# Rows out of a spectral filter, scattered to experts one tile at a time instead of chunk by chunk

## The chip, the cores and the metric

The kernel runs on one core of a Trainium2 chip. Its engines are PE (matrix products), DVE and ACT (vector and scalar work), POOL (here mostly scatters) and SP (which issues transfers). The metric is the device time of one execution in microseconds (us); lower is better. The time before is 1450.88 us, the median of three runs (1448.48 to 1457.94).

## The reference, cut to what matters

Eight batches of 2496 tokens with 256 channels go through a filter in frequency space, and every row of the result then goes through one of eight experts, the one whose normalised embedding is nearest:

```python
def _attn_ref(x, filt_r, filt_i):                 # x: 8 x 2496 x 256
    X = np.fft.rfft(x, axis=1)
    F = (filt_r + 1j * filt_i)[None, :, :]
    return np.fft.irfft(X * F, n=x.shape[1], axis=1).astype(np.float32)

def _moe_ref(x, expert_emb, tau, w1, w2):         # x: 19968 x 256, 8 experts, 1024 hidden
    xn = x / (np.linalg.norm(x, axis=-1, keepdims=True) + 1e-06)
    en = expert_emb / (np.linalg.norm(expert_emb, axis=-1, keepdims=True) + 1e-06)
    logits = xn @ en.T / tau
    expert_idx = np.argmax(logits, axis=1)
    ...
    gate_w = probs[np.arange(N), expert_idx]      # softmax of the logits, at the largest
    for e in range(E):
        mask = expert_idx == e
        h = np.maximum(x[mask] @ w1[e], 0.0)
        out[mask] = gate_w[mask, None] * (h @ w2[e])
```

## The kernel before, in words

**Groups and stages.** Each batch is a group of its own; there are eight groups, 0 to 7. The filter of a group takes three steps: `conv_s1` (39-point transform along b), `conv_s2` (64-point transform along a, product with the filter, and back) and `conv_sb` (back along b). `conv_sb` works in 11 tiles of two halves of 117 rows each; a half is what the text calls a row tile of the scatter, and 22 of them make a group. For each tile it writes the rows as two 16-bit halves of a number into a `rows` tile, with the token's number from a POOL `iota` (L571), has them transposed by a transfer (`yT`, L537), and computes logits (L595).

**Routing.** After four tiles (a *chunk*; eight row tiles, in the last chunk of a group six) `route` does the rest for all of them at once on DVE: softmax, first largest expert, and the place of each row within its expert's region of the buffer `XS` in memory (`ix`, L664). The places are cast to integers `ixi` (L666), the output scales go into the rows (L678), and POOL scatters each row tile to `XS` with an indirect transfer (L687, `scatter_rows`). `route` is a generator, and `part()` in `conv_sb` advances it by one `yield`; `part()` is called twice for each tile, once per *half step*, and then until nothing is left. Between two `yield`s of `route` stand two scatters. There are 22 scatters per group in chunks of 8, 8 and 6, 176 in all, and eight more of empty rows at the end of group 7 (`zero_rows`).

**Slots.** When a group's filter ends, its rows are cut into *slots*, blocks of 256 rows of one expert (128 for the first group and for the last blocks). A slot loads its rows transposed (`xT`, by SP, from `XS`) and goes through its expert in four units (quarter slots). A unit has a copy of a quarter of the first weights on DVE (`wp`, L808, `prep`), the first product on PE (`ph`, L820), its positive part and remainder `h` on ACT (L826) and DVE (L827), and the second product on PE (`po`, L840). After the fourth unit ACT scales each 128 rows into a result tile `o` (L847), and POOL scatters it to the output (L848).

**What sets the order.** `run_slots` runs through the slots of all groups so far, and `spread`, called twice per unit, lays steps of the next group's filter between them: each step has a weight, and `pace` divides the steps' weight by the units that are left in the queue, so that the next group's filter ends just before the slots run out. PE's and ACT's instructions stay in the order of the program; DVE's, POOL's and SP's are ordered by a scheduler, which takes an instruction when its inputs are ready by its own reckoning. `behind("dve")` binds an instruction to a place behind the last weight copy issued so far (`last["dve"]`, set in `prep`). Pools hold the tiles: `rowp` 9 row tiles (a pool that the filter's parts `ap`, `yp` also use), `mp2` two of each of its tags, among them `o`.

Of the kernel before, what the change touches and what calls it, by code (L numbers as in the profile page):

```python
# [15 lines left out]
I32 = mybir.dt.int32  # L16
# [8 lines left out]
NA, NB39 = 64, 39          # sequence length 2496 = 64 * 39  # L25
S = NA * NB39
NK2 = 20                   # frequencies 0..19 of the 39-point transform
A3 = 3                     # a's in one token tile
TOK = A3 * NB39            # 117 tokens in a tile
NAG = (NA + A3 - 1) // A3  # 22 tiles in a batch, the last with one a  # L30
# [3 lines left out]
ROW = 516                  # hi 256, lo 256, token id, output scale  # L34
# groups of batches whose filter is done together; the rows of the slots that come after each
GROUPS = ((1, 128),) + ((1, 256),) * 7
CW = 2 * D                 # columns in a tile: two batches, or two places of one batch
CHUNK = 4                  # tiles of columns in a routing chunk
NTC = 2 * CHUNK
XYB, INB, CYB = 6, 4, 3    # buffers of the filter's products, of its inputs, of transposed rows  # L40
W_S1, W_S2, W_SB, W_GAP = 0.8, 1.0, 1.3, 2.5  # weights of the filter's steps between slots
MARGIN = 3                 # quarter slots that the filter of a group ends early
SAL, LPL = 2, 3            # tiles that lie between a step of the filter and the products that use it
# groups from which a transform takes its products by parts: there, back along b, a, and back along a
G_S1, G_SB, G_S2, G_SA = 2, 3, 4, 3
DLAG = 2                   # units between the two products of a unit
MID = 8                    # matrix products of a unit before the next slot's registers are loaded
WLOADS = {3: 1, 6: 1, 10: 2, 32: 2} | {n: 1 for n in range(12, 32, 2)}  # loads of weights at the first group's steps
WLATE = 6                  # experts whose halves follow their scales at once
PT = 1                     # half of a tile of the first group that the tensor engine transposes  # L50


def full_blocks(tokens, size):
    """Blocks of `size` rows that are full in E regions with `tokens` rows in all, at the least."""
    return max(0, -((E * (size - 1) - tokens) // size))
# [3 lines left out]
def moe_spectral_kernel(  # L59
# [25 lines left out]
    # phases: after which group, rows in a slot, slots  # L85
# [17 lines left out]
    rowp = ctx.enter_context(tc.tile_pool(name="rowp", bufs=9))  # L103
# [33 lines left out]
    # 8 - e, e * CAP, token ids, slot numbers  # L137
# [10 lines left out]
    # 1 where the partition holds a token, in a full tile and in the last one of a batch  # L148
# [9 lines left out]
    def norm_eps(out_, ssq, tmp):  # L158
        """sqrt(max(ssq, 1e-30)) + 1e-6 by Newton steps for the inverse root; ssq is clamped in place."""
# [25 lines left out]
    ent = const.tile([P, 2, 2 * E], F16, tag="ent", name="ent")   # per half of the channels: hi, lo  # L185
    enz = const.tile([P, 2, 2 * E], F16, tag="enz", name="enz")   # hi, 0
# [23 lines left out]
    def weight_loads():  # L210
        """The raw weights of an expert lie a place ahead of their halves, the last ones aside."""
# [16 lines left out]
    def weight_halves():  # L228
        """Powers of two that take the largest terms to [64, 128) and [2**14, 2**15); then the halves."""
# [57 lines left out]
    def tiles(g, t):  # L287
        """(batch, a-group) of the two halves of the t-th tile of columns."""
        n, _ = GROUPS[g]
        return [(first[g] + j, t) if n == 2 else (first[g], 2 * t + j) for j in range(2)]  # L290
# [4 lines left out]
    # e * CAP + rows so far  # L295
    state = {"base": ecap}

    def widths(g):
        """Tiles of columns in the transforms along b, and along a."""
        return NAG * GROUPS[g][0] // 2, NK2 * GROUPS[g][0] // 2  # L300


    def whole(g, ap, t, rows, full):
        """The parts of tile t of a tensor in memory: (half or both, partitions, memory)."""
# [38 lines left out]
    def split(hi, lo, pieces):  # L343
        """High and low parts of the pieces of a tile."""
# [13 lines left out]
    def asides(nm):  # L358
        """Room for parts in two tiles for rows."""
# [3 lines left out]
    def parts_of(c, tag):  # L363
        """A constant's high part in its place, and its low part."""
# [9 lines left out]
    def product(out_, c, a):  # L374
        """c times a tile's piece, in float32 or by parts."""
# [8 lines left out]
    def conv_s1(g):  # L384
        """39-point transform along b."""
# [19 lines left out]
    def conv_s2(g):  # L405
        """64-point transform along a, filter, and back."""
# [18 lines left out]
        def filtered(out_, in_, fts, ri):  # L425
            """in_ times the filter's real part, or times the sign and its imaginary part."""
# [21 lines left out]
        for k in range(NK + lag):  # L448
            if k + INB - 1 < NK:
                ain[k + INB - 1] = load_a(k + INB - 1)  # L450
            if k < NK:
# [6 lines left out]
                # real and imaginary halves change places  # L458
# [10 lines left out]
                else:  # L469
                    # while the first group is alone, the tensor engine has the time for the sum  # L470
# [22 lines left out]
    def conv_sb(g):  # L493
# [15 lines left out]
        def part():  # L509
            if parts and next(parts[0], None) is None:  # L510
                parts.pop(0)
# [530 lines left out]
```

## Time and profile before

| | |
|---|---|
| median of three runs | 1450.88 us (1448.48 to 1457.94) |
| profiled execution: span from first to last instruction | 1551.4 us |
| the profiled execution's own time | only its span is recorded, 100.5 us above the median |
| mean granted clock of PE | 0.901 |
| busy: PE, DVE, ACT, POOL | 83%, 64%, 48%, 36% |
| row scatters (L687) | 176, 179.2 us, 1018 ns each on average |
| result scatters (L848) | 161, 170.6 us, 1060 ns each |
| weight copies (L808) | 384, 190.8 us, 497 ns each |
| casts of places (L666) | 24, 0.166 us each (median) |

The profile is of one execution on the chip. Busy times are those of an engine's instructions; waits are idle times before an instruction with what ended them, its releaser. "issue" as a releaser means that the engine waited for nothing that the profile shows; "remote" means that it was released by something that the profile can't name. A row of the waits reads: engine, operation and line, releaser, total us, times, longest. In a window the number in brackets behind a busy time counts instructions. Line numbers are those of the kernel before; in the changed kernel the same statements stand a few lines lower (L687 is L693, L808 is L814, L848 is L854).

In time, the span has three parts: group 0 alone to 213 us; the filters of groups 1 to 7 beside slots of earlier groups to about 1316 us; slots alone to the end.

### The profile page before, as it was taken

Reading aid. Unit: us, or ns where it says so; the run is one execution under the profiler, and the core shown is the slowest. Engines: PE = TensorE matmul, PEld = TensorE weight load, DVE = VectorE, ACT = ScalarE, POOL = GpSimd, SP = SyncE. Lnnn points to the kernel's source line nnn. Section 1 sums busy time; section 2 is a strip of 40 time slices with the busy share of each in tenths; the row PEclk is TensorE's granted clock in tenths of the full one; section 3 lists DMA queues with packets and bytes.
Section 4 is the critical chain, followed back from the end, with each engine's and each line's share of the span. In section 5 each row is a group of like instructions: output and inputs, shape, how many; then the busy total and the mean of one; then the engine's idle time right before and its main releaser. Section 6 shows DMA issues by size and latency. Waiting matters only on the chain.

```text
span 1551.4 us, 35680 instructions
## 1 busy us (share of the span) xinstructions
PE 1281.1 (83%) x10370; PEld 970.5 (63%) x10370; DVE 992.8 (64%) x3086; ACT 747.8 (48%) x1704; POOL 552.5 (36%) x613
## 2 busy tenths in 40 slices
PE   4543668878876987898988998998899977999996
PEld 1111335654654665676767776776678865888996
DVE  3775766746666665686758774877578844444563
ACT  2654535524642665366536663666356721323332
POOL 0112454145335323552435334542453145112221
PEclk7766779988987998999989998999999997999998
DMA  8873779757975787576847795769566742222121
GB/s 278 326 260 90 173 230 226 155 146 212 243 166 162 202 174 173 158 210 173 187 124 201 185 202 132 207 188 195 131 172 191 140 100 86 48 56 49 40 50 30
DMA packets 320794, 250.96 MB, mean 162 GB/s; under 512 B 215865, under 2 KB 262273, under 8 KB 318821
## 3 DMA queue, kind: packets, MB, share of 16 engines
q1 hardware_dynamic: 290044, 171.48, 45.9%
q0 software_dynamic: 26400, 60.07, 13.6%
q10 hardware_dynamic: 4169, 17.12, 3.1%
q8 instruction: 99, 1.62, 0.4%
q14 instruction: 82, 0.67, 0.1%
HBM read 121.61 MB, written 84.84 MB: 133 GB/s over the span
## 4 chain that ended last, share of the span: by engine, by line
PE 54%; issue 15%; DMA 13%; DVE 9%; ACT 4%; POOL 2%; another core or an unknown queue 2%; SPq 0%; DVEq 0%; POOLq 0%; ACTq 0%
PE ph L820 20%; PE po L840 19%; DMA yT<-rows 5%; PE s L382 4%; PE s L377 3%; DMA f<-ZD 2%; PE y L382 2%; DMA ZD<-z 2%; PE y L377 2%; POOL out_dram L848 2%; PE sa L382 2%; PE sa L486 2%; DVE xs L434 1%; PE lp L595 1%
## 5 line engine op out<-in xcount | busy, mean ns | idle before, releaser
L820 PE MATMUL ph<-xT,wp 128*128 128x256 f16 (+1 forms) x4608 | 529.3, 263 | 42.4 <-issue 21.0
L840 PE MATMUL po<-W,h 128*128 x3864 | 522.4, 281 | 25.7 <-issue 24.4
L820 PEld LDWEIGHTS <-wp 128*128 128x128 f16 x4608 | 394.7, 100 | 138.5 <-issue 66.7
L840 PEld LDWEIGHTS <-h 128*128 128x128 f16 x3864 | 374.6, 100 | 119.0 <-issue 66.8
L826 ACT ACTIVATE h<-ph 128x512 f16<-128x512 f32 (+1 forms) x384 | 203.6, 532 | 348.6 <-PE ph L820 190.7
L808 DVE COPY wp<-W 128x1024 f16 x384 | 190.8, 497 | 207.0 <-PE ph L820 131.5
L848 POOL DMA_INDIRECT out_dram<-o,meta x161 | 170.6, 1060 | 397.0 <-ACT o L847 351.3
L827 DVE SCALAR_TENSOR_TENSOR h<-ph,h 128x512 f16<-128x512 f32 (+1 forms) x384 | 230.1, 599 | 58.2 <-ACT h L826 56.0
L687 POOL DMA_INDIRECT XS<-rows,ixi x176 | 179.2, 1018 | 175.1 <-issue 109.0
L468 POOL TENSOR_TENSOR yy<-yy,xs 128x512 f32<-128x512 f32 x70 | 95.7, 1371 | 130.9 <-DVE xs L434 95.2
L337 POOL DMA_DIRECT2D in<-in_x x84 | 66.5, 792 | 153.2 <-DVE xp L351 68.5
L847 ACT ACTIVATE o<-po,meta 128x256 f32<-128x256 f32 x161 | 69.4, 475 | 48.2 <-PE po L840 26.4
L562 ACT ACTIVATE rows<-y 128x256 f16<-128x256 f32 x176 | 66.5, 389 | 50.4 <-PE y L377 29.6
L432 DVE TENSOR_TENSOR yy<-s,f 128x256 f32<-128x256 f32 x160 | 61.4, 415 | 43.8 <-ACT xs L461 27.8
L530 ACT ACTIVATE rows<-y,rr 128x256 f16<-128x256 f32 x176 | 74.6, 479 | 27.1 <-DVE rr L567 24.8
L533 DVE SCALAR_TENSOR_TENSOR rows<-y,rr,rows 128x256 f16<-128x256 f32 x176 | 76.8, 476 | 15.6 <-ACT rows L530 13.4
L460 ACT COPY xs<-s 64x512 f32<-64x512 f32 x80 | 46.6, 583 | 74.8 <-PE s L377 50.7
L377 PE MATMUL s<-a,c_sb 128*128 128x512 f32 x80 | 53.0, 756 | 32.5 <-issue 15.1
L434 DVE SCALAR_TENSOR_TENSOR xs<-xs,sgn_sb,f 128x256 f32<-128x256 f32 x160 | 77.3, 519 | 0.0
L377 PE MATMUL y<-f,csb_sb 120*128 120x512 f32 (+2 forms) x72 | 43.5, 693 | 37.2 <-issue 21.2
L400 ACT COPY s<-s 128x512 f32<-128x512 f32 x88 | 52.1, 593 | 39.3 <-DMA SD<-s 13.0
L595 PEld LDWEIGHTS <-yT 128*128 128x128 f16 x704 | 36.0, 100 | 55.8 <-DMA yT<-rows 35.1
(189 smaller groups left out, 1520.7 us busy)
## 6 DMA issues: line engine op xcount, KB each, us to landing
f<-in_filt SPq DMA_DIRECT2D x160, 256.0 KB
a<-SD SPq DMA_DIRECT2D x80, 256.0 KB
ZD<-z SPq DMA_DIRECT2D x80, 256.0 KB
SD<-s SPq DMA_DIRECT2D x80, 240.0 KB
f<-ZD SPq DMA_DIRECT2D x80, 240.0 KB
in<-in_x POOLq DMA_DIRECT2D x70, 234.0 KB
W<-in_w ACTq DMA_DIRECT2D x14, 1024.0 KB
XS<-rows,ixi POOLq DMA_INDIRECT x176
```

Of the source, the lines that this page charges most:

```text
L377: nc.tensor.matmul(out_, c[:a.shape[0]], a, start=True, stop=True)
L382: nc.tensor.matmul(out_, w[:k], b, start=(n == 0), stop=(n == 2))
L434: nc.vector.scalar_tensor_tensor(out=o, in0=i, scalar=sgn_sb[:, k2:k2 + 1], in1=f, op0=ALU.mult, op1=ALU.mult)
L468: nc.gpsimd.tensor_tensor(out=yy, in0=yy, in1=xs, op=ALU.add)
L533: nc.vector.scalar_tensor_tensor(out=rows[:, i, D:2 * D], in0=y[:, i], scalar=rr[:, u:u + 1], in1=rows[:, i, 0:D], op0=ALU.mult, op1=ALU.s ...
L687: i = nc.gpsimd.indirect_dma_start(out=XS, out_offset=bass.IndirectOffsetOnAxis(ap=ix, axis=0), in_=src, in_offset=None)
L808: last["dve"] = nc.vector.tensor_copy(wp, src[:, :, fp * 256:fp * 256 + 256])
L820: last["pe"] = nc.tensor.matmul(ph[:, fi, :size], wp[:, k * 2 + wh, fi * P:(fi + 1) * P], xT[:, xh * 2 + k], start=(c == 0), stop=(c == 5))
L826: nc.scalar.activation(h[:, 0, :, :size], ph[:, :, :size], AF.Relu)
L827: nc.vector.scalar_tensor_tensor(out=h[:, 1, :, :size], in0=ph[:, :, :size], scalar=0.0, in1=h[:, 0, :, :size], op0=ALU.max, op1=ALU.subtract)
L840: nc.tensor.matmul(self.po[:, s], self.hs[fp][:, hh, fi, s * P:(s + 1) * P], self.Wp[:, off + wh * 1024:off + wh * 1024 + D], start=(fp == ...
L848: i = nc.gpsimd.indirect_dma_start(out=out, out_offset=bass.IndirectOffsetOnAxis(ap=self.meta[:, s, 0:1].bitcast(I32), axis=0), in_=o, in_ ...
```

## The change

`route` no longer scatters. For each row tile it puts a function `rows_out` on a list, and `part()`, at each half step, also takes one from the list: it casts that tile's one column of places, behind the last weight copy issued so far, and scatters it. So a half step sends one row tile where a step of `route` sent two, the 24 casts of 128x8 (or 128x6) become 176 of 128x1, and the half steps after a group's last tile, five before, are ten. `ix` moves to a pool with three buffers. `o` has four tiles instead of two, `rowp` eleven instead of nine, the scratch memory of the dynamic transfers has 8 KB instead of the default 16, and `pace` counts three more half steps. All comments are gone too, which changes line numbers only.

```diff
-    rowp = ctx.enter_context(tc.tile_pool(name="rowp", bufs=9))
+    rowp = ctx.enter_context(tc.tile_pool(name="rowp", bufs=11))
...
-        parts = []
+        parts, out_rows = [], []
...
         def part():
             if parts and next(parts[0], None) is None:
                 parts.pop(0)
+            if out_rows:
+                out_rows.pop(0)()
...
-                    parts.append(route(g, **ck))
+                    parts.append(route(g, out_rows, **ck))
             yield W_SB
-        while parts:
+        while parts or out_rows:
             part()
             yield W_SB
...
-        ix = sm("ix")
+        ix = rt.tile([P, NTC], F32, tag="ix", name=f"ix{tg}")[:, :nt]
         v.tensor_reduce(out=ix, in_=pos, axis=AX.X, op=ALU.add)
         ixi = rt.tile([P, NTC], I32, tag="ixi", name=f"ixi{tg}")[:, :nt]
-        v.tensor_copy(ixi, ix)
...
+        def rows_out(u, k):
+            with behind("dve"):
+                v.tensor_copy(ixi[:, u:u + 1], ix[:, u:u + 1])
+            scatter_rows(g, rows[u // 2][:k, u % 2].bitcast(I32), ixi[:k, u:u + 1])
+
         for u, (_, ag) in enumerate(of):
-            k = tokens(ag)
-            scatter_rows(g, rows[u // 2][:k, u % 2].bitcast(I32), ixi[:k, u:u + 1])
-            if u % 2 and u < nt - 1:
-                yield 1
+            out_rows.append(lambda u=u, k=tokens(ag): rows_out(u, k))
...
-                    o = mp2.tile([P, D], F32, tag="o", name=f"o{self.nm}_{s}")
+                    o = mp2.tile([P, D], F32, tag="o", bufs=4, name=f"o{self.nm}_{s}")
...
-            steps = 2 * W_S2 * (nk + SAL) + W_SB * (2 * ntl + 8 + 2 * LPL) + W_S1 * nxt + 4 * W_GAP
+            steps = 2 * W_S2 * (nk + SAL) + W_SB * (2 * ntl + 11 + 2 * LPL) + W_S1 * nxt + 4 * W_GAP
...
-    nc = bacc.Bacc("TRN2", target_bir_lowering=False, num_devices=1)
+    nc = bacc.Bacc("TRN2", target_bir_lowering=False, num_devices=1, dynamic_dma_scratch_size=8192)
```

The order of instructions on DVE and POOL comes from the scheduler, so it is shown at three places. A row has the line, the operation, and output and inputs; in `ixi6_4_15812` 6 is the group, 4 the first tile of the chunk, the last number a running one.

DVE before, in group 6 behind the second chunk's places (`ix6_4`), while the slots of group 5 run (`wp5_6_1` is unit 1 of slot 6 of that phase):

```order
L664 TENSOR_REDUCE ix6_4_15810<-l6_4_15806 128x8
L666 CAST ixi6_4_15812<-ix6_4_15810 128x8
L808 ISA
L808 COPY wp5_6_1_15895<-W_197 128x1024
L827 SCALAR_TENSOR_TENSOR h5_5_3_15867<-ph5_5_3_15854,h5_5_3_15867 128x512
L808 ISA
L808 COPY wp5_6_2_15958<-W_197 128x1024
L625 COPY l6_8_15935<-lp6_8_15768 128x48
```

and DVE in the changed kernel at the same place:

```order
L667 TENSOR_REDUCE ix6_4_15931<-l6_4_15927 128x8
L686 CAST ixi6_4_15933<-ix6_4_15931 128x1 x3
L814 ISA
L814 COPY wp5_6_1_16015<-W_197 128x1024
L686 CAST ixi6_4_15933<-ix6_4_15931 128x1 x2
L833 SCALAR_TENSOR_TENSOR h5_5_3_15987<-ph5_5_3_15974,h5_5_3_15987 128x512
L814 ISA
L814 COPY wp5_6_2_16080<-W_197 128x1024
...
L686 CAST ixi6_4_15933<-ix6_4_15931 128x1
...
L814 COPY wp5_6_3_16183<-W_197 128x1024
L686 CAST ixi6_4_15933<-ix6_4_15931 128x1 x2
```

One cast of eight columns has become eight of one, three ahead of the copy for unit 1, two behind it, one behind unit 2's, and two behind unit 3's.

DVE in the changed kernel in group 3, first chunk:

```order
L814 COPY wp2_5_2_7662<-W_197 128x1024
L686 CAST ixi3_0_7299<-ix3_0_7297 128x1 x4
L570 TENSOR_SCALAR rr3_8_7324<-q3_8_7332 128x2
L351 TENSOR_TENSOR xp4_7_1_7514<-in4_7_7070,xp4_7_0_7513 117x512
L686 CAST ixi3_0_7299<-ix3_0_7297 128x1 x2
L166 SCALAR_TENSOR_TENSOR n03_4_7610<-sg3_4_7609 128x8
L686 CAST ixi3_0_7299<-ix3_0_7297 128x1
L833 SCALAR_TENSOR_TENSOR h2_5_0_7603<-ph2_5_0_7590,h2_5_0_7603 128x512
...
L686 CAST ixi3_0_7299<-ix3_0_7297 128x1
...
L814 COPY wp2_5_3_7789<-W_197 128x1024
```

Here all eight stand between two weight copies. In groups 1 to 3 that holds for seven of nine chunks; in groups 4 to 7 the casts of all twelve stand on both sides of one to three weight copies, and in three of the twelve (5_0, 5_4 and 7_4) five or six of them stand together. In group 0 there are no slots yet.

POOL before, in group 3 at its first chunk (`o2_4_0` is the first 128 rows of slot 4 of the phase before):

```order
L848 DMA out_0_dram<-o2_4_0_7589,meta2_4_6928 19968x256
L848 DMA out_0_dram<-o2_4_1_7594,meta2_4_6928 19968x256
L687 DMA XS_220<-rows3_0_6499,ixi3_0_7356 161920x258 x2
L687 DMA XS_220<-rows3_1_6591,ixi3_0_7356 161920x258 x2
L687 DMA XS_220<-rows3_2_6712,ixi3_0_7356 161920x258 x2
L687 DMA XS_220<-rows3_3_6786,ixi3_0_7356 161920x258 x2
L571 IOTA rows3_9_7481 128x2
L571 IOTA rows3_10_7607 128x2
```

and POOL in the changed kernel there:

```order
L574 IOTA rows3_9_7458 128x2
L693 DMA XS_220<-rows3_0_6543,ixi3_0_7299 161920x258 x2
L693 DMA XS_220<-rows3_1_6630,ixi3_0_7299 161920x258 x2
L693 DMA XS_220<-rows3_2_6747,ixi3_0_7299 161920x258 x2
L574 IOTA rows3_10_7552 128x2
L693 DMA XS_220<-rows3_3_6812,ixi3_0_7299 161920x258 x2
L854 DMA out_0_dram<-o2_4_0_7746,meta2_4_7031 19968x256
L854 DMA out_0_dram<-o2_4_1_7751,meta2_4_7031 19968x256
```

The eight scatters stay neighbours on POOL; the result scatters of slot 4 have moved from ahead of them to behind them, and the token numbers of tiles 9 and 10 from behind them to among them.

More of the change, by code (lines that the diff above doesn't have):

```diff
@@ L604, in conv_sb, with route @@
             yield from zero_rows(state["base"])
-    def route(g, t0, n, rows, ssq, rr, lp):
+    def route(g, out_rows, t0, n, rows, ssq, rr, lp):
         tg = f"{g}_{t0}"
```

## The prediction

> **What bounds the kernel now.** I read the span and the engine shares first, then the chain that ended last, the waits, and the stretches of the program by engine.
>
> ```profile
> core 0: 1551.4 us, clock 0.901
> PE 1281.1 (83%) x10370; PEld 970.5 (63%) x10370; DVE 992.8 (64%) x3086; ACT 747.8 (48%) x1704; POOL 552.5 (36%) x613
> PE 54%; issue 15%; DMA 13%; DVE 9%; ACT 4%; POOL 2%; another core or an unknown queue 2%; SPq 0%; DVEq 0%; POOLq 0%; ACTq 0%
> 1316.00:1430.00 114.00, 114.00 (x1043) 101.99 (x1041) 52.48 (x94) 34.42 (x64) 20.32 (x21) 1.00 0.23 52
> ```
>
> The last row is a window of the tail, where only slots are left; its first figure behind the length is PE's busy time. PE works 114.00 of 114.00 us there, and nothing in the change takes a product away. So whatever the change gains lies before 1316 us, where PE waits.
>
> The rows out are scattered by POOL in trains. Here are the last three scatters of one train of eight, and what PE, ACT and DVE do around its end (start, length, what, idle time before it and its releaser):
>
> ```profile
> 1276.40 0.98 POOL L687 DMA_INDIRECT XS<-rows,ixi  x1 [0.30 <-issue]
> 1277.12 0.27 PE L820 MATMUL ph<-xT,wp 128*128 128x256 f16 x1 [1.06 <-issue]
> 1277.68 0.98 POOL L687 DMA_INDIRECT XS<-rows,ixi  x1 [0.30 <-issue]
> 1278.51 0.49 PE L820 MATMUL ph<-xT,wp 128*128 128x256 f16 x3 [1.13 <-issue]
> 1278.97 0.98 POOL L687 DMA_INDIRECT XS<-rows,ixi  x1 [0.30 <-issue]
> 1280.25 1.01 POOL L848 DMA_INDIRECT out_dram<-o,meta  x1 [0.30 <-issue]
> 1284.24 0.43 DVE L808 COPY wp<-W 128x1024 f16 x1 [8.83 <-remote]
> 1284.30 1.08 ACT L826 ACTIVATE h<-ph 128x512 f16<-128x512 f32 x2 [8.62 <-remote]
> ```
>
> A scatter takes 0.98 us and the next follows 0.30 us later, so a chunk's eight take about 10 us, with the result rows (`out`) queued behind. From the sixth scatter on PE issues products singly or by threes with gaps of about a microsecond, and ACT and DVE get word of finished products only after the train, both at 1284.3. Over the run these late releases carry the name "remote":
>
> ```profile
> ACT h L826 <- remote: 70.8, 13, 10.2
> DVE wp L808 <- remote: 45.9, 8, 8.8
> ```
>
> How much of PE's time that costs is read from windows, first those that hold the twelve trains of groups 4 to 7, then the four long stretches between them; then the same for groups 1 to 3 (sum rows):
>
> ```profile
> sum 173.00, PE 130.41 PEld 98.17 DVE 79.17 ACT 58.25 POOL 111.18; mean PE 10.87 PEld 8.18 DVE 6.60 ACT 4.85 POOL 9.27
> sum 407.00, PE 385.92 PEld 308.08 DVE 323.22 ACT 278.15 POOL 143.81; mean PE 96.48 PEld 77.02 DVE 80.81 ACT 69.54 POOL 35.95
> sum 128.00, PE 85.50 PEld 61.82 DVE 56.91 ACT 35.59 POOL 81.79; mean PE 9.50 PEld 6.87 DVE 6.32 ACT 3.95 POOL 9.09
> sum 193.00, PE 169.12 PEld 119.70 DVE 131.09 ACT 113.42 POOL 61.74; mean PE 84.56 PEld 59.85 DVE 65.54 ACT 56.71 POOL 30.87
> ```
>
> In groups 4 to 7 PE is idle 42.6 of 173 us inside the trains (24.6%) and 21.1 of 407 us between them (5.2%). At the second rate the trains would have lost 9.0 us, so their excess is 42.6 - 9.0 = 33.6 us. In groups 1 to 3 it is 42.5 - 0.124 x 128 = 26.6 us. Together 60.2 us hang on the trains; that is the prize.
>
> **How the profile stands to the times.** The profiled execution spans 1551.4 us against a median of 1450.88, so it carries 100.5 us (6.9%) that a timed one doesn't have. PE's tail has no idle time to give back, so the 100.5 us sit before it, and the 60.2 us of train excess are the largest single lump that could be missing there. PE's idle time before 1316 us is 1316 less its busy time there (1281.1 - 222.5 in the tail), 257.4 us. If every idle microsecond shrinks alike, 1 - 100.5/257.4 = 61% of each is left in a timed execution; if the trains give first, nothing is left of them. The Trainium skill, "Runtime: NRT & Kernel Launch", section "The ~15µs preamble/postamble breakdown", gives a fixed gap of about 6.2 us between the two times; the 100.5 us here are far from that, so the measurement decides.
>
> **The change part by part.**
>
> *Rows out, one per half step.* The 176 scatters stay, 0.98 us each; only their dates move. A scatter now stands behind the cast of its own column, and the cast behind the last weight copy issued before it. In the order of DVE, seven of the nine chunks of groups 1 to 3 still have all casts between two weight copies: the train stays, and I take 0 of the 26.6 us. In groups 4 to 7 nine of the twelve chunks are split into pieces of at most four between weight copies; three keep five or six together. In the tail window PE ran 1043 products, and a 256-row slot has 96: 10.9 slots in 114 us, 10.5 us each, 2.6 us for a quarter slot with its one weight copy. A piece of two scatters fills 2 x 1.28 = 2.56 of it, so POOL is nearly as full as in a train, though a train's sixth scatter comes later. Bounds: all 33.6 us gained, or 18 lost (176 scatters, each in the way of a copy for the 0.10 us that the last row below is longer than the mean). I take half of 33.6, -17 us. On POOL the scatters now stand among the token numbers and the result scatters, and what follows there (inputs, sums `yy`) waits for one scatter at a time where it waited for a train. Next late, where a train goes, are the transposed rows, a wait that the chain holds inside a train too:
>
> ```profile
> 789.00 4.71 DMA yT<-rows
> 789.05 0.99 POOL L687 DMA_INDIRECT XS<-rows,ixi  x1 [5.42 <-DVE wp L808]
> 792.92 0.98 POOL L687 DMA_INDIRECT XS<-rows,ixi  x1 [0.30 <-issue]
> 793.52 0.60 DVE L808 COPY wp<-W 128x1024 f16 x1 [3.64 <-PE po L840]
> ```
>
> The last row is also what a simpler cause would have to explain: a weight copy that runs in the middle of a scatter, in 0.60 us against 0.497 on average (group row below). So copy and scatter do not shut each other out here. By the Trainium skill, "SBUF — State Buffer", section "Who interferes with whom", a DVE copy in a two-port mode and a GpSimd instruction hold the shared ports exclusively, and PE and ACT never wait. By that rule a copy would lose at most one scatter, and ACT's 70.8 us of "remote" would not be there; this trace speaks against it as the cause of the crawl.
>
> *Casts.* 24 casts of 128x8 become 176 of 128x1, and each must be done before its scatter.
>
> ```profile
> L666 DVE CAST ixi<-ix x24: 151/166/176, 173.8 to 1289.0; 128x8 int32<-128x8 f32 x16, 128x6 int32<-128x6 f32 x8
> L808 DVE COPY wp<-W 128x1024 f16 x384 | 190.8, 497 | 207.0 <-PE ph L820 131.5
> ```
>
> 152 more at no more than 0.166 us are 25 us of DVE time. DVE is 64% busy and holds 9% of the chain; 9% of 25 is +2 us. Bounds 0 and +25. Behind a cast on DVE stand the next `h` and the next weight copy; both lose at most a few casts, under 1 us.
>
> *Four result tiles, eleven row tiles.* A result tile is free again when its scatter is out. What waited for tiles before:
>
> ```profile
> ACT o L847 <- remote: 16.9, 6, 5.6
>   PE po L840: 0.8, 1
>   ACT rows L562: 9.2, 3
> POOL out_dram L848 <- ACT o L847: 351.3, 63, 15.9
> ```
>
> ACT's `o` sat 16.9 us behind trains (inside term one as far as it moved PE), PE waited 0.8 us for `o`; rows of the ninth and later tiles waited 9.2 us for scatters (who waited for the row tiles). POOL itself waits 351.3 us for `o`, so results are not held up by POOL as a whole. I take -2 for the results (0 to -16.9) and -2 for the rows (0 to -9.2); both are wanted by the pacing, since `o` scatters now queue behind scatters that wait for casts.
>
> *Later group ends.* After a group's last tile the program makes ten half steps instead of five, and `pace` counts three more (3 x 1.3 = 3.9 of about 90 in weight). Counted through the program's loops, a group's slots join the queue at quarter slots 45, 66, 102, 142, 179, 219, 265 where it was 44, 64, 103, 142, 178, 217, 265: no more than two quarter slots late, 5.2 us, and a slot or none is left in the queue at the join, as before. The group's first loads must wait for the last scatter. Before, that showed only here:
>
> ```profile
>   PE ph L820: 4.3, 2
> ```
>
> (who waited for `XS`). I take 0, bounds 0 and +10.5 (a whole slot). *The 8 KB scratch* I take at 0: scatters 0.98 us long and 0.30 apart show no wait for room at the old size. If half the room made each wait for the one before to land, 176 scatters would last perhaps twice as long, 172 us more of POOL, which is busy 36% of the span and so has room for it off the path; the far end is the slower rival's +21.
>
> **The sum.** In the profile's time: -17 + 2 - 2 - 2 + 0 = -19 us. A timed execution keeps between 61% of that (-12) and, if the trains vanish there, only +2 - 2 - 2 = -2. I take the middle nearer the first, -11: 1450.9 - 11 = **1440 us**.
>
> **The rivals.** *Stalls as real as in the profile, and broken up.* Then the whole -33.6 + 2 - 2 - 2 = -36 us comes at best and -19 at least: 1415 to 1432, about 1424. For it: the waits named remote are long and regular in all long trains. Against: the 100.5 us that timed executions don't have.
>
> *It doesn't do what it says.* POOL runs the pieces one after the other, since casts of a chunk lie close together, or the stall isn't there without the profiler: -2 to +3 us, 1449 to 1454, the middle 1451. For it: the unbroken trains of groups 1 to 3; against: the 3 to 5 pieces per chunk later.
>
> *Slower: the join.* The last scatter of a group is issued five half steps later; these weigh 1.3 each at a pace of about 2.2 per quarter slot, so 5 x 1.3 / 2.2 x 2.6 = 7.7 us. At seven joins with one slot or none left in the queue, PE runs dry where the lead of the last scatter over the next slot's first product was less than 7.7 us. In the trace of before it was short twice (4.3 us above). If it decides at three joins, 3 x 7.7 = 23, less the -2 of the rest: 1472 us. Two more buffers don't help, since it is a date and not a room. Against it: `pace` gives 3.9 of the 6.5 back, by running the filter 4% faster.
>
> **How the numbers follow.** A difference of 1% (14.5 us) is about what a measurement of this kernel can tell from no change; faster means under 1436.4, slower over 1465.4. Chances: forecast 0.40 (1432 to 1448, a quarter of it under 1436.4), stalls real 0.28 (all faster), nothing happens 0.16 (all within), slower 0.16 (1462 to 1482, nearly all over 1465.4, so 0.15). Faster 0.28 + 0.10 = 0.38; slower 0.15; within 0.47. The range leaves out about a tenth at each end: 1418, inside the stalls' own range, and 1466, inside the slower rival's.
>
> **What would show it.** In the profile after: POOL's scatters of groups 4 to 7 in pieces of two or three with weight copies between; the late releases named remote under a third of 70.8 and 45.9 us; PE's idle share in the corresponding stretches of groups 4 to 7 nearer 15% than 25%; casts of about 0.16 us, 176 of them; `o` no longer held; the tail still full. The forecast is wrong if the remote waits go and the timed median stays (the stall was the profiler's), if they stay in pieces too, or if PE waits for `xT` for over 10 us at the joins.

## The result, and the profile after

The changed kernel takes 1416.77 us (median of four runs, 1405.92 to 1420.96) where the kernel before takes 1450.01 beside it: a ratio of 0.9742, 95% interval 0.9689 to 0.9795. It is faster by 2.6%, over three times the 0.75% that was forecast, and just below the range. The kernel before runs in one of two conditions, at 1447 to 1468 us or at 1547 to 1577, which all runs of a comparison share; by its span the profile before was taken in the second, the profile after in the first.

The page of the profile after, with the core's line first:

```profile
core 0: 1419.0 us, clock 0.939
PE 1224.2 (86%) x10370; PEld 950.6 (67%) x10370; DVE 987.4 (70%) x3238; ACT 749.1 (53%) x1704; POOL 552.5 (39%) x613
PE 39%; DMA 13%; issue 6%; ACT 3%; DVE 3%; POOL 2%; SPq 0%; POOLq 0%; DVEq 0%; ACTq 0%
```

The chain holds no "another core or an unknown queue" any more, and no wait of this profile is named remote. It looks as if the stalls had been broken up. But in this profile a chunk's scatters mostly follow one another as before; these are POOL's of the first chunk of group 7:

```profile
1141.90 1.24 POOL L693 DMA_INDIRECT XS<-rows,ixi  x1 [0.88 <-issue]
1143.45 0.99 POOL L693 DMA_INDIRECT XS<-rows,ixi  x1 [0.30 <-DVE sg L170]
1144.74 0.99 POOL L693 DMA_INDIRECT XS<-rows,ixi  x1 [0.30 <-issue]
...
1147.40 0.97 POOL L693 DMA_INDIRECT XS<-rows,ixi  x1 [0.31 <-issue]
1148.68 1.13 POOL L693 DMA_INDIRECT XS<-rows,ixi  x1 [0.30 <-DVE n L162]
1150.12 0.97 POOL L693 DMA_INDIRECT XS<-rows,ixi  x1 [0.30 <-issue]
1151.40 0.98 POOL L693 DMA_INDIRECT XS<-rows,ixi  x1 [0.30 <-DVE h L833]
```

Eight in 10.5 us, with the same 0.30 us between them: the train is there, and nothing is late behind it. In groups 1 to 7, 5 of the 133 scatters that follow another of their chunk start more than 2 us after it, where it was 1 of 133. So the two profiles may not be laid side by side, and the first question was what belongs to the change and what to the condition.

### The profile page after: what moved, and what is told of

The parts are those of the page before. It is cut to its first block, busy times and chain, and to the rows that moved or that the text cites. A ratio compares the mean times of both kernels' runs of the same rounds, so it can differ in the third digit from the quotient of the medians.

```text
span 1419.0 us, 35828 instructions
## 1 busy us (share of the span) xinstructions
PE 1224.2 (86%) x10370; PEld 950.6 (67%) x10370; DVE 987.4 (70%) x3238; ACT 749.1 (53%) x1704; POOL 552.5 (39%) x613
## 4 chain that ended last, share of the span: by engine, by line
PE 39%; DMA 13%; issue 6%; ACT 3%; DVE 3%; POOL 2%; SPq 0%; POOLq 0%; DVEq 0%; ACTq 0%
PE ph L826 16%; PE po L846 15%; DMA yT<-rows 7%; DMA out_dram<-o,meta 3%; PE s L382 3%; PE sa L382 2%; DMA f<-ZD 2%; PE y L382 2%; POOL out_dram L854 1%; PE lp L598 1%; DVE h L833 1%; POOL yy L468 1%; DMA a<-SD 0%; DVE xs L434 0%; ACT vp L350 0%
## 5 line engine op out<-in xcount | busy, mean ns | idle before, releaser
L826 PE MATMUL ph<-xT,wp 128*128 128x256 f16 (+1 forms) x4608 | 509.1, 258 | 5.1 <-DVE h L833 2.3
L846 PE MATMUL po<-W,h 128*128 x3864 | 498.1, 274 | 0.9 <-DVE h L833 0.9
L826 PEld LDWEIGHTS <-wp 128*128 128x128 f16 x4608 | 387.5, 99 | 86.4 <-issue 36.7
L846 PEld LDWEIGHTS <-h 128*128 128x128 f16 x3864 | 366.3, 98 | 73.4 <-issue 28.5
L814 DVE COPY wp<-W 128x1024 f16 x384 | 186.8, 487 | 141.0 <-PE ph L826 134.1
L693 POOL DMA_INDIRECT XS<-rows,ixi x176 | 182.7, 1038 | 113.9 <-issue 53.1
L377 PE MATMUL s<-a,c_sb 128*128 128x512 f32 x80 | 49.1, 707 | 36.4 <-issue 14.3
```

Of the source, the lines that this page charges most:

```text
L377: nc.tensor.matmul(out_, c[:a.shape[0]], a, start=True, stop=True)
L693: i = nc.gpsimd.indirect_dma_start(out=XS, out_offset=bass.IndirectOffsetOnAxis(ap=ix, axis=0), in_=src, in_offset=None)
L814: last["dve"] = nc.vector.tensor_copy(wp, src[:, :, fp * 256:fp * 256 + 256])
L826: last["pe"] = nc.tensor.matmul(ph[:, fi, :size], wp[:, k * 2 + wh, fi * P:(fi + 1) * P], xT[:, xh * 2 + k], start=(c == 0), stop=(c == 5))
L846: nc.tensor.matmul(self.po[:, s], self.hs[fp][:, hh, fi, s * P:(s + 1) * P], self.Wp[:, off + wh * 1024:off + wh * 1024 + D], start=(fp == ...
```

## The experiments

Each ratio below is to the kernel before, run beside it on the same chip, with its 95% interval.

### The profile of before again, and the change beside it

The kernel before was profiled three more times (no edit), and the changed one once more.

> The kernel before, once more, for a second profile of it. The profile shown first spans 1551 us where its timed runs take 1450. If the late releases in the trains of scatters are a feature of this kernel, this profile shows them again (remote: 70.8 us on ACT, 45.9 on DVE before) in a span near 1550; if they belong to that one execution, the span is about 1450 and the waits named remote fall to a fraction, under 25 us on ACT, and the 33 us that the change won must be found in other rows of this profile.

> The changed kernel once more, beside the kernel before on the same chip. The chip of the first runs gave 1554 to 1561 us for the kernel before and long late releases; the chip of the result gave 1450. If the change breaks up the stalls, it takes back more where they are long: 1561 falls to 1420 to 1480, and no wait is named remote. If the late releases belong to a chip and not to the order of the scatters, they stay (60 us and more on ACT) and the ratio is the same as on the other chip, about 0.974: near 1521 where before takes 1561.

> The kernel before, a third profile. If this chip gives the kernel about 1450 us, the profile shows what that time consists of: by the theory that late releases belong to a chip, no wait named remote over 5 us, and PE's idle share in the trains of groups 4 to 7 near that between them. By the theory that they belong to the kernel, 20 us or more of them even so. On a chip that gives 1555 it shows them as before.

> The kernel before, a profile beside runs near 1455 us, as the last four kernels had. If the late releases belong to the condition in which this kernel takes 1555 us, none is named remote here for more than 5 us, and PE's idle time beside the scatters of groups 1 to 7 is well under the 78 us of the first profile, but above the 28 us of the changed kernel (35 to 50). If they belong to the trains, 20 us or more are named remote.

The kernel before took 1554.14, 1569.51 and 1567.35 us in these three, beside medians of 1561.40, 1565.71 and 1564.51. The first profile, at 1551.4 us, was no odd execution, then; it fits an ordinary one of the slower condition. The changed kernel took 1525.95 beside 1565.71: 0.9743 (0.9658 to 0.9828), the same ratio as in the faster condition. Two profiles of that comparison can be laid side by side, the third of before and the one of the change (core lines, then the waits named remote, before first):

```profile
core 0: 1567.6 us, clock 0.892
ACT h L826 <- remote: 73.5, 15, 7.8
DVE wp L808 <- remote: 57.5, 13, 7.4
```

```profile
core 0: 1530.2 us, clock 0.913
ACT h L832 <- remote: 89.3, 19, 9.4
DVE wp L814 <- remote: 71.5, 14, 9.0
```

The change doesn't shorten the late releases at all (69.2 to 82.3 us on ACT's `h` in four profiles of before), and it is still 2.6% faster. The hope for a profile of before in the faster condition failed (the fourth fell in the slower one), so whether late releases occur there with the kernel before stays open; with the changed kernel and three of its variants none did.

The rows did come apart here. In groups 4 to 7 of the change (e5) 15 of the 76 scatters that follow another of their chunk start over 2 us after it, in nine of the twelve chunks; the three others are 5_0, 5_4 and 7_4, the very ones in which the order on DVE keeps five or six casts together. In the four profiles of before there is none such in these groups, and in the profile after there are 3. These sum rows are of twelve windows, each from a chunk's first scatter to the end of its last, in groups 4 to 7 (third profile of before, then the change):

```profile
sum 112.70, PE 93.04 PEld 73.93 DVE 49.10 ACT 36.79 POOL 89.23; mean PE 7.75 PEld 6.16 DVE 4.09 ACT 3.07 POOL 7.44
sum 147.50, PE 121.32 PEld 95.83 DVE 79.69 ACT 49.23 POOL 93.70; mean PE 10.11 PEld 7.99 DVE 6.64 ACT 4.10 POOL 7.81
```

PE is idle 19.7 of 112.7 us (17%) before and 26.2 of 147.5 (18%) with the change, so the gaps took nothing from its idle time. How a gap opens can be seen in the first chunk of group 6, around its sixth and seventh scatter:

```profile
1085.37 0.98 POOL L693 DMA_INDIRECT XS<-rows,ixi  x1 [0.30 <-issue]
1086.36 1.08 PE L846 MATMUL po<-W,h 128*128 x3 [0.64 <-issue]
1087.93 0.43 DVE L814 COPY wp<-W 128x1024 f16 x1 [5.90 <-remote]
1087.99 0.60 ACT L832 ACTIVATE h<-ph 128x512 f16<-128x512 f32 x1 [7.53 <-remote]
1088.28 0.15 DVE L686 CAST ixi<-ix 128x1 int32<-128x1 f32 x1
1089.25 0.99 POOL L693 DMA_INDIRECT XS<-rows,ixi  x1 [2.90 <-issue]
```

Six scatters go out as a train, PE issues its products with gaps, and the weight copy is released late; the next cast stands behind that copy, and the seventh scatter behind the cast. In this chunk the late release opens the gap, so the gap can't have prevented it.

Where the 37 us between these two spans lie is read from windows, summed over groups 1 to 7: first the stretches from a group's last scatter to the next one's first, then those from the first scatter of a group to its last. Before:

```profile
sum 728.00, PE 660.90 PEld 501.98 DVE 536.02 ACT 454.41 POOL 250.71; mean PE 94.41 PEld 71.71 DVE 76.58 ACT 64.92 POOL 35.82
sum 374.00, PE 293.64 PEld 221.01 DVE 194.64 ACT 120.24 POOL 187.36; mean PE 41.95 PEld 31.57 DVE 27.81 ACT 17.18 POOL 26.77
```

and the change:

```profile
sum 702.00, PE 642.28 PEld 486.80 DVE 533.66 ACT 459.00 POOL 245.84; mean PE 91.75 PEld 69.54 DVE 76.24 ACT 65.57 POOL 35.12
sum 363.00, PE 290.40 PEld 225.46 DVE 203.44 ACT 116.12 POOL 189.29; mean PE 41.49 PEld 32.21 DVE 29.06 ACT 16.59 POOL 27.04
```

26 us of the gain lie between the trains and 11 in the stretches that hold them; PE's idle time falls by 7.4 and 7.8 us there. (Ahead of these windows the change is 7 us longer, behind them 7 us shorter.) The rest is PE's busy time: over the whole run it is 1293.6 us before and 1276.1 with the change for the same 10370 products, at a granted clock of 0.892 and 0.913. The timed runs of this comparison bear the clock out: 0.910 to 0.915 in the four of the change, 0.888 to 0.900 in the thirteen of before. In the faster condition (e13) it is 0.932 to 0.940 against 0.919 to 0.933. So a higher clock goes with the change; whether it is a cause of the gain or follows from PE's shorter waits is not shown.

### Room: scratch, result tiles, row tiles

Of the three edits to the kernel before, e2 has the first, e6 the first and second, e7 the first and third, e3 and e18 all:

```diff
-    nc = bacc.Bacc("TRN2", target_bir_lowering=False, num_devices=1)
+    nc = bacc.Bacc("TRN2", target_bir_lowering=False, num_devices=1, dynamic_dma_scratch_size=8192)
...
-    rowp = ctx.enter_context(tc.tile_pool(name="rowp", bufs=9))
+    rowp = ctx.enter_context(tc.tile_pool(name="rowp", bufs=11))
...
-                    o = mp2.tile([P, D], F32, tag="o", name=f"o{self.nm}_{s}")
+                    o = mp2.tile([P, D], F32, tag="o", bufs=4, name=f"o{self.nm}_{s}")
```

> The kernel before with the 8 KB scratch for dynamic transfers and nothing else; its instructions stand in the same order on every engine. If the size of the scratch limits how many scatters are under way at once and that is what sped the kernel up, this alone gives 1417 to 1430 us. If the pacing did it, the time stays at 1450 (1443 to 1457). If the smaller scratch costs something that the change hid, it is slower, over 1460.

> The kernel before with the 8 KB scratch and four result tiles, nine row tiles. If result tiles carry the buffers' gain, since ACT then never waits with a scaled result for a scatter behind a train, the ratio is 0.985 to 0.990; if the row tiles do, 0.998.

> The kernel before with the 8 KB scratch and eleven row tiles, two result tiles. Buffers together gave a ratio of 0.987, the scratch alone 0.998. If row tiles carry it (waits of the row tiles for scatters were 9 to 17 us), 0.985 to 0.990; if the result tiles do, 0.998.

> The kernel before with 8 KB scratch, four result tiles and eleven row tiles; rows still go out chunk by chunk, and instructions stand in the same order on every engine. By the theory of the prediction (the trains hurt, buffers are worth 2 + 2 us) 1446 us, within 1443 to 1453. If the buffers carry the gain, 1417 to 1430.

> The kernel before with 8 KB scratch, four result tiles and eleven row tiles, as in the third run, where the ratio was 0.987 beside a kernel before of 1561 us. If the buffers' share doesn't hang on the late releases, 0.984 to 0.990; if they only help where releases come late, 0.993 to 1.003.

| kernel | us | before | ratio |
|---|---|---|---|
| scratch (e2) | 1557.00 | 1561.40 | 0.9977 (0.9940 to 1.0014) |
| result tiles (e7) | 1548.37 | 1565.71 | 0.9925 (0.9885 to 0.9966) |
| row tiles (e6) | 1538.64 | 1565.71 | 0.9848 (0.9776 to 0.9920) |
| all three (e3) | 1542.09 | 1561.40 | 0.9871 (0.9815 to 0.9926) |
| all three (e18) | 1542.21 | 1564.51 | 0.9855 (0.9791 to 0.9920) |

The row tiles carry it; the result tiles alone are worth about half as much and add nothing that can be seen to the row tiles. e18 was meant for the faster condition and fell in the slower one, so it is a repeat of e3. One thing in e3's expectation is wrong: eleven row tiles do change the order, because the scheduler lets an instruction wait for a free tile by its own reckoning. POOL in group 1, the kernel before (-) against e3 (+):

```
 L571 IOTA rows_8_3065 128x2
 L848 DMA out_dram<-o_6_0_3016,meta_6_2508 19968x256
+L571 IOTA rows_9_3156 128x2
+L571 IOTA rows_10_3270 128x2
 L687 DMA XS<-rows_0_2299,ixi_0_3038 161920x258 x2
...
 L848 DMA out_dram<-o_7_0_3286,meta_7_2724 19968x256
-L571 IOTA rows_9_3156 128x2
-L571 IOTA rows_10_3270 128x2
```

A group has eleven tiles. With nine buffers, tiles 9 and 10 need the buffers of tiles 0 and 1, so their first write waits for the first chunk's scatters, and the steps of tile 9 on DVE and ACT come later with it. ACT then sat before `rows` until scatters had landed (third profile of before, who waited for the row tiles):

```profile
  ACT rows L562: 13.6, 4
```

No such row is there in e3, e6 or the change. In the six profiles of the kernel before and of it with other sizes but nine row tiles this wait is 9 to 17 us, less than the 24 that the row tiles are worth (1.5% of 1565.71); the rest went with the order, and what in the order is not shown. The filter's `ap` and `yp` come from the same buffers, which is a rival that was not separated: PE's weight loads for `sa` waited 8.4 to 10.6 us for `yp` in those six profiles and 2.9 in e3, e6 and e18.

### The paced rows without the room, and with parts undone

All start from the changed kernel. e12 has the first of these edits, e15 the second, e4 both and the old scratch (with the one more that its expectation names); e9 has only the third, which frees the casts from the weight copies; e13 has none:

```diff
-    rowp = ctx.enter_context(tc.tile_pool(name="rowp", bufs=11))
+    rowp = ctx.enter_context(tc.tile_pool(name="rowp", bufs=9))
...
-                    o = mp2.tile([P, D], F32, tag="o", bufs=4, name=f"o{self.nm}_{s}")
+                    o = mp2.tile([P, D], F32, tag="o", name=f"o{self.nm}_{s}")
...
-            with behind("dve"):
-                v.tensor_copy(ixi[:, u:u + 1], ix[:, u:u + 1])
+            v.tensor_copy(ixi[:, u:u + 1], ix[:, u:u + 1])
```

> The changed kernel with the old sizes: two result tiles, nine row tiles, 16 KB scratch (and six buffers for the slots' row data where there were eight, to make room for 64 bytes). If pacing alone is the gain, 1417 to 1425 us. If it needs the buffers, since result scatters now queue behind scatters that wait, 1435 to 1470. If the buffers carry all of it, 1450.

> The changed kernel with nine row tiles instead of eleven. A group has eleven tiles; with nine, the last two wait until the first scatters of their own group are out, and paced scatters are out later. If that is what keeps the pacing alone at 0.998, the ratio is 0.990 to 1.000, with ACT's rows waiting for XS again; if the result tiles do it, 0.974 to 0.980.

> The changed kernel with two result tiles instead of four. Alone they were worth 0.75%; nine row tiles in the change gave 0.988 where all gives 0.974. If result tiles matter with paced rows as much, 0.980 to 0.988; if not, 0.972 to 0.978.

> The changed kernel, but the casts of a column are not bound behind the last weight copy; in the order of DVE a chunk's casts then mostly stand together again (eight or six in a row in eight of the twelve chunks of groups 4 to 7). If setting the scatters apart by weight copies carries the pacing's share, the ratio to before goes from 0.974 to about 0.987, that of the buffers alone. If it is the dates and the room and not the binding, it stays at 0.970 to 0.978.

> The changed kernel again, beside the next three on one chip, in more rounds. Its ratio was 0.974 on two chips, with an interval that touches those of the kernels with one part undone (0.985 to 0.988). If each part carries its share, 0.970 to 0.978 with an interval under 0.982; if the 0.974 was the lucky end, 0.980 to 0.986.

| kernel | us | before | ratio |
|---|---|---|---|
| the change, more rounds (e13) | 1415.02 | 1455.50 | 0.9737 (0.9689 to 0.9786) |
| with two result tiles (e15) | 1425.79 | 1455.50 | 0.9779 (0.9719 to 0.9839) |
| casts unbound (e9) | 1553.53 | 1572.00 | 0.9853 (0.9805 to 0.9900) |
| with nine row tiles (e12) | 1551.18 | 1572.00 | 0.9883 (0.9842 to 0.9924) |
| with the old sizes (e4) | 1560.55 | 1561.40 | 0.9983 (0.9948 to 1.0019) |

The whole change is 1.2 to 1.3% better than the room alone. The intervals are just apart (to 0.9786, from 0.9791) for e13 and e18, which are of different conditions; within the slower one, e5's reaches to 0.9828 and they overlap. That three measurements of the change all give 0.974 speaks for the difference. Paced rows on the old room gain nothing, but e4 also has two buffers fewer for the slots' row data, whose cost was not measured. Nine row tiles cost the change 1.4%, about as much as eleven are worth alone, and ACT waits 8.3 us for `XS` again. Two result tiles cost it 0.4%, inside the intervals. Binding the casts is worth some 1.2%: without it the ratio is that of the room alone, though e9's interval overlaps e5's. In e9 1 of the 76 scatters of groups 4 to 7 stands apart (15 in e5). Its late releases, and the sum row of its twelve chunks there, are these:

```profile
ACT h L831 <- remote: 126.2, 23, 10.8
DVE wp L813 <- remote: 93.2, 20, 10.9
sum 112.80, PE 77.97 PEld 58.23 DVE 40.09 ACT 22.96 POOL 89.22; mean PE 6.50 PEld 4.85 DVE 3.34 ACT 1.91 POOL 7.43
```

With the binding (e5) the late releases are 89.3 and 71.5 us, and PE is idle 18% of these stretches where it is 31% here (34.8 of 112.8 us). In these two traces the binding takes back late releases that the rest of the change adds; against the kernel before nothing is left of it. That late releases set the time is not shown: e10 below, which is bound too, has 67.0 us of them on ACT's `h`, the least of the paced kernels in the slower condition, and nearly the ratio of e9.

### The count in pace, and one row per weight copy

The first edit is e16's; e10 has 8 there, and e11 is the kernel before with all the room and 11. e14 has 18 there and the second edit, by which a row waits for a weight copy behind which no row of its group stands yet, or for four half steps:

```diff
-            steps = 2 * W_S2 * (nk + SAL) + W_SB * (2 * ntl + 11 + 2 * LPL) + W_S1 * nxt + 4 * W_GAP
+            steps = 2 * W_S2 * (nk + SAL) + W_SB * (2 * ntl + 14 + 2 * LPL) + W_S1 * nxt + 4 * W_GAP
...
             if out_rows:
-                out_rows.pop(0)()
+                now = last.get("dve")
+                if now is None or now is not sent[0] or sent[1] >= 4:
+                    sent[:] = [now, 0]
+                    out_rows.pop(0)()
+                else:
+                    sent[1] += 1
```

> The changed kernel with the old count in pace (8 half steps instead of 11), so the filter runs some 4% slower beside the slots and a group ends later. If the count matters (the slower rival's mechanism: slots run dry at the joins) the ratio rises from 0.974 to 0.985 or more. If the queue never runs dry, 0.970 to 0.978.

> The changed kernel with 14 half steps in the count of pace instead of 11 (with 8 the ratio was 0.986). If the count has to match the half steps that there are (39 or 38 against 39 counted) and the filter running ahead costs, 0.980 to 0.990. If more is simply better, since queues then never run dry, 0.965 to 0.974. If the differences of a per cent come from how the order falls out, anything from 0.97 to 0.995.

> The kernel before with the buffers (8 KB scratch, four result tiles, eleven row tiles) and the new count in pace, rows still out chunk by chunk. If running the filter 4% faster beside the slots is the pacing's share, 0.970 to 0.978; if it is the rows' way out, 0.985 to 0.990 as with the buffers alone.

> The changed kernel, but a half step sends a row tile only if a weight copy has been issued since the last one (or after four half steps without one), so that nearly every cast of a chunk stands behind a copy of its own; pace counts 18 half steps. If trains of scatters cause the late releases, those named remote fall from 89 us on ACT to under 50, and the ratio to 0.95 to 0.97. If the late releases don't hang on how scatters stand to each other, they stay at 70 to 100, and the later group ends cost: 0.975 to 1.00.

| kernel | us | before | ratio |
|---|---|---|---|
| the change, count 8 (e10) | 1547.95 | 1572.00 | 0.9860 (0.9823 to 0.9897) |
| the change, count 14 (e16) | 1437.88 | 1455.50 | 0.9867 (0.9804 to 0.9930) |
| the room, count 11 (e11) | 1568.84 | 1572.00 | 0.9989 (0.9953 to 1.0024) |
| one row per weight copy (e14) | 1460.92 | 1455.50 | 1.0032 (0.9995 to 1.0068) |

Three half steps more in the count cost the change 1.3% (e16, beside e13), three fewer about as much (e10, whose interval touches that of e5 in its condition), and three more cost the room alone 1.2 to 1.3%. PE waits 8.1 us for `xT` in e16 (0.2 in e13) and 3.9 in e10 (0.6 in e5), which is a part of it at most. The reading that the count must match the half steps that there are fits the change (39 counted, 38 there by the program's loops) but not the chunks, which do better with 36 counted for 33 than with 39. So whether 11 is right for a reason or fell well by chance stays open; a program whose order comes from a scheduler can move by a per cent for either.

e14 was to spread the scatters and to show what late releases become. It fell in the faster condition, where none is named remote, so it says nothing on them. It does price the slower rival. 46 of the 133 scatters that follow another of their chunk start over 2 us after it (5 in e13), group ends come later, and slots wait for their rows. PE's row among those who waited for `xT`, and the chain's pieces over 3.4 us on `XS` and `xT`:

```profile
  PE ph L831: 16.3, 3
306.34 4.01 DMA xT<-XS
620.65 5.03 DMA XS<-rows,ixi
757.61 3.77 DMA XS<-rows,ixi
921.62 4.47 DMA XS<-rows,ixi
926.15 3.43 DMA xT<-XS
1041.13 7.13 DMA XS<-rows,ixi
1055.48 4.84 DMA XS<-rows,ixi
1231.77 3.72 DMA xT<-XS
```

These pieces are 36.4 us together; in e13's chain two such pieces are 8.3. The difference, 28 us, stands against 38.0 us between the two spans (1450.0 and 1412.0). In e13 PE's wait for `xT` is 0.2 us, once.

## Why the prediction was wrong

**The discount, the step that failed first.** "The profile carries 100.5 us that a timed one doesn't have", and so half of the gain was struck off. The 100.5 us were the condition, not the profiler: in every run whose profile and time are both known they agree (1419.0 us span and 1420.96 us; 1552.3 and 1554.14), and the kernel before takes 1547 to 1577 us unprofiled, too. By the Trainium skill, "Runtime: NRT & Kernel Launch", section "The ~15µs preamble/postamble breakdown", a profile's total time lies a constant of some 6 us above the reported time; here the span lies 1.7 to 2.1 us below it, so size and sign differ, but the gap is small and nearly constant. A gap of 100 us should therefore have led to the conclusion that profile and times were not of one condition. Without the discount the sum was -19 us in the profile's terms, 1.2% of 1551, still less than half of the 39.8 us measured in that condition.

**Rows out, -17 us from late releases in groups 4 to 7.** The reading of the order held in the slower condition, and what was to follow from it did not. In the slower condition the scatters come apart in the nine chunks that the prediction counted, but the late releases are 89.3 us on ACT with the change and 69 to 82 in four profiles before it, and PE is idle 18% of those stretches where it was 17%. In the chunk shown, the first six scatters still go as a train and PE slows down within it; the gap opens only behind a weight copy that is already late. By the prediction's own sign, remote waits that stay though the scatters are in pieces, the step fails. In size -17 us comes close to what pacing is worth on top of the room (1.2% of 1450 is 17 us), but by luck: that share is lost without the binding and with either change of the count, and what carries it stays open.

**Eleven row tiles, -2 us (bounds 0 to -9.2).** The term that was mis-sized most: -1.5% alone (with the scratch, which is worth nothing that can be seen), 24 us of 1566. The step priced a wait by its row and left out that the scheduler orders by free tiles; how much each of the two, and of the shared buffers of `ap` and `yp`, makes of the 24 us is not shown.

**Four result tiles, -2 us (0 to -16.9).** About -12 us alone (5 to 18), inside the bounds; in the change 0.4%, not told from nothing.

**Later group ends, 0 (0 to +10.5), and the count in pace.** No slot runs dry in the change (0.2 to 1.4 us of waits for `xT`), as forecast. But the count was taken to be worth nothing, and three half steps off it cost 1.2 to 1.3%.

**The 8 KB scratch at 0** holds: 0.9977 (0.9940 to 1.0014). **The casts**: 144 ns each (median of 176), near the 0.166 assumed; their +2 us was not measured by itself.

**The rivals.** The time came out at the lower end of "stalls as real as in the profile", 1415 to 1432, but not by its mechanism. "It doesn't do what it says" was right that the late releases would not be broken up, wrong on the trains in the slower condition, where they do come apart, and wrong on its time. The join's price was right in kind: in e14 it shows in some 28 us of the chain.

**On the kernel before**, the text said that PE's and ACT's instructions stay in program order; the kernel's fixed order (`manual_schedule`) holds for group 0 alone. Behind it the scheduler orders them too, so a small edit can move every engine's order.

## What to carry to other kernels

Before a profile is laid against timed runs, compare its span with its own time: if they agree and the median doesn't, the runs are of another condition, and nothing in the trace may be discounted for it. Where a scheduler orders by free buffers, a wait for a buffer is only the visible part of what the buffer is worth; count how many tiles are alive at once (here eleven in a group) and give that many before moving the work that frees them. And undo each part of a change by itself: here paced rows, worth nothing on the old room, were worth 1.2% on top of the new, and undoing the binding or the count alone brought the ratio back to that of the room. Last, that a stall and a train stand together doesn't show which comes first: look at what released the instruction at the gap.

## What the runs showed of the hardware

In one condition ACT and DVE learn of finished products late: ACT's waits for `h` named remote are 57 to 126 us in each of fifteen profiles (of the kernel before, the change and variants of both), the longest 13.3 us (e10, e11). In the other no wait is named remote, with trains as dense (five profiles, of the change and its variants). Between them lie over 100 us for the kernel before (medians of 1450 and 1455 against 1561 to 1572 us), at two times on one chip as well (1455 and 1572), and the ratio of the change is 0.974 in both.

The late releases are not the whole difference. The granted clock of the kernel before is 0.886 to 0.905 in its timed runs of the slower condition and 0.919 to 0.933 beside e13, in the faster one. PE is busy 1276.1 us with the change in e5 and 1224.2 in the profile after, for the same products: 52 of the 111 us between the two spans. What causes the condition was not tested.

The Trainium skill, "SBUF — State Buffer", section "Who interferes with whom", says that PE and ACT never wait on anyone, as a rule on the ports of that memory. The late releases are waits for a signal that the profile can't name; that any of them is a wait for a port is not shown, so these runs don't decide on that rule.
